# A three-stage chain (decayed attention, dense layer, routed experts) on one core: late tiles of 64 + 64 rows from two experts

## The chip, the cores and the metric

One Trainium2 chip, of which the program uses one core. The metric is the device time of one execution in microseconds (us). Engines are named as in the profile: PE (TensorE matmul), PEld (its weight load), DVE (VectorE), ACT (ScalarE), POOL (GpSimd), SP (SyncE, here the queue that starts most DMAs).

## The reference, cut to what matters

```python
state = gamma * state + einsum('bhd,bhe->bhde', k[:, :, t], v[:, :, t])     # attention, 768 steps
y[:, :, t] = einsum('bhd,bhde->bhe', q[:, :, t], state) / sqrt(D)
...
h = x @ w_in                                       # 3072 x 512 by 512 x 2048
x = (maximum(h, 0) + log1p(exp(-abs(h)))) @ w_out
...
expert_idx = argmax(x @ w_gate, axis=1)            # 8 experts, one per token
for e in range(E):
    mask = expert_idx == e
    h = maximum(x[mask] @ w1[e], 0)                # 512 x 1024
    out[mask] = gate_w[mask, None] * (h @ w2[e])   # 1024 x 512
```

For the inputs that setup_inputs() draws the eight experts get, from the largest to the smallest, 1441, 647, 291, 270, 230, 89, 74 and 30 of the 3072 tokens.

## The kernel before, in words

All matmul operands are f16. A number is held as a high and a low half, and a product is three matmuls (high by high, high by low, low by high). Attention and the dense layer run first, mixed with each other. The kernel then forms the experts' work as **slots** of 128 token rows. Experts are taken in **turns** by size, turn 0 being the largest. A slot holds rows of one turn only, so each turn's last slot is partly empty.

A table in DRAM lists each expert's tokens in the order in which they were routed; `rank` scatters into it. `early_pick` takes four early slots (j = -4 to -1) from turns 0 and 1 before all tokens are routed. After the last tokens `slots_pick` (on DVE) counts each turn's blocks of 128 rows and computes where each of the remaining slots starts; `fetch` (POOL) reads their token lists from the table, and `spread` transposes them on PE and copies them to `idsT` and `gateT`. `NSURE` late slots always run, and an If behind them runs the others up to `NSLOT` when the flag `more` is set. With the counts above the late slots are 8, 6, 3, 3, 2, 1, 1 and 1 by turn, 25 in all, which is NSURE.

A slot's steps: `gather(j)` (POOL) collects its 128 rows from `x2d`; `turn(j)` transposes them into xT by DMA on SP; `layer1(j)` is 24 matmuls of 512 columns on PE in two halves (12 each), each half followed by r and hb on ACT (lines 381 and 383) and the low half of hb on DVE (384); then a DMA transpose of hb into hT on SP (386); `layer2(j)` is 24 more matmuls; DVE scales and POOL scatters the rows to the output (398, 399). In the main loop layer2(j - 2) follows layer1(j). PE's order is written by hand.

Weights: `ring` has four parts, each one expert's w1 (half 0) and w2 (half 1). `Direct` loads the first four experts in 32 units of 512 KB (`raw`, six buffers) and splits each into high and low on ACT (133) and DVE (134) in the same stretch in which the early slots run. The loads' and the splits' places are positions counted in PE matmuls. The other four experts are split earlier and kept in `wsp`; `load_next` copies 2 MB halves of them into the ring part that the preceding turn has left, when turn 1, 2, 3 or 4 begins. It is issued for every slot with a condition `go`, and its three register values are read by SP (408 to 410).

`in_line` fixes the order of SP's DMAs in the late part as the order in which the code calls them. A list `ticks` says after which matmul of the early slots the helper steps are called: 42 `rank`, 44 `slots_pick`, 116 `spread`, the gathers of slots 0 to 2 and the turns of slots 0 and 1.

Of the kernel before, what the change touches and what calls it, by code (L numbers as in the profile page):

```python
# [8 lines left out]
F32 = mybir.dt.float32  # L9
# [11 lines left out]
P = 128  # L21
# [4 lines left out]
E = 8  # L26
# [10 lines left out]
NSLOT = NT // P + E - 1  # L37
NSURE = 25
RING = 4
TROWS = E * NT + 32 * P  # L40
# [18 lines left out]
def moe_chain(ctx, tc, q, k, v, moe_w_in, moe_w_out, moe2_w_gate, moe2_w1, moe2_w2, cst, cst16, out, dbg=None):  # L59
# [28 lines left out]
    for n in (16, 4, 8, P, E, E, 1, 32, NT // P):  # L88
        cols.append(cs[:, at0:at0 + n])
        at0 += n  # L90
    dec, zd, zd8, mask, rev, base, iota_p, iota_j, tok = cols
# [25 lines left out]
    halved = []  # L117
# [18 lines left out]
    class Direct:  # L136
# [13 lines left out]
        def at(self, pos, after):  # L150
# [8 lines left out]
            while self.m < self.n and self.SPLIT[self.m] <= pos:  # L159
# [14 lines left out]
    idsE = const.tile([P, NEARLY], U32, name="idsE")  # L174
    gateE = const.tile([P, NEARLY], F32, name="gateE")
    rg = const.tile([1, 3, 32], U32, name="rg")
# [7 lines left out]
    nblk = const.tile([P, 1], F32, name="nblk")  # L184
    cc = [const.tile([P, 2 * E], F32, name="c%d" % i) for i in range(4)]
    late = []

    def reclaim(x):

        tc.add_manual_dep(nc.gpsimd.drain().ins, x.name, NOSYNC, reason="order")  # L190
# [6 lines left out]
    def fetch(n, blk_u):  # L197
        nc.gpsimd.indirect_dma_start(
            out=late[1][0:n].rearrange("p r c -> p (r c)"), out_offset=None, in_=table.rearrange("(b r) c -> b (r c)", r=P),
            in_offset=bass.IndirectOffsetOnAxis(ap=blk_u[0:n, :], axis=0), bounds_check=TROWS // P - 1, oob_is_err=True)  # L200

    def spread(n, ids, gates):
        ps = ps_at.tile([P, 2, 32], F32, tag="at", name="idt")
        for i in range(2):
            nc.tensor.transpose(ps[:, i, 0:n], late[1][0:n, :, i], ident[0:n, 0:n])
        nc.vector.tensor_copy(out=ids, in_=ps[:, 0, 0:n])
        nc.vector.tensor_copy(out=gates, in_=ps[:, 1, 0:n])
# [7 lines left out]
    def turns_pick():  # L215
# [14 lines left out]
        nc.vector.tensor_scalar(out=kblk, in0=expert, scalar1=float(NT // P), scalar2=None, op0=ALU.mult)  # L230
        nc.vector.memset(taken, 0.0)
        nc.vector.memset(nblk, float(E * NT // P))
# [3 lines left out]
    def early_pick():  # L236
        ps = counts()
        t = r_p.tile([P, E, E], F32, tag="byt", name="byt", bufs=1)
        ns = r_p.tile([P, E], F32, tag="start", name="ns")
# [3 lines left out]
        ab32 = r_p.tile([P, 2], U32, tag="ab32", name="ab32", bufs=1)  # L243
        ab = r_p.tile([P, 2], F32, tag="ab", name="ab", bufs=1)
        a, b = ab[:, 0:1], ab[:, 1:2]
        nc.vector.tensor_copy(out=ab32, in_=ns[:, 0:2])
        nc.vector.tensor_scalar(out=ab32, in0=ab32, scalar1=7, scalar2=None, op0=ALU.logical_shift_right)
        nc.vector.tensor_scalar(out=ab, in0=ab32, scalar1=float(NEARLY), scalar2=None, op0=ALU.min)
        nc.vector.tensor_scalar(out=b, in0=b, scalar1=a, scalar2=float(NEARLY), op0=ALU.add, op1=ALU.min)
        d = r_p.tile([P, 2], F32, tag="pm", name="d")  # L250
        c = r_p.tile([P, 2], F32, tag="blk2", name="c", bufs=1)
        blk = r_p.tile([P, 1], F32, tag="blk", name="blk")
        blk_u = r_p.tile([P, 1], U32, tag="blku", name="blku")

        nc.vector.scalar_tensor_tensor(out=d[:, 0:1], in0=kblk[:, 1:2], scalar=kblk[:, 0:1], in1=a, op0=ALU.subtract, op1=ALU.subtract)
        nc.vector.scalar_tensor_tensor(out=d[:, 1:2], in0=a, scalar=kblk[:, 1:2], in1=nblk, op0=ALU.subtract, op1=ALU.add)
# [4 lines left out]
        fetch(NEARLY, blk_u)  # L261
        nc.vector.tensor_scalar(out=rP, in0=iota_j[0:1, 0:NEARLY], scalar1=a[0:1], scalar2=RING - 1.0, op0=ALU.is_lt, op1=ALU.mult)
        nc.vector.tensor_copy(out=taken[:, 0:1], in_=a)
        nc.vector.tensor_tensor(out=taken[:, 1:2], in0=b, in1=a, op=ALU.subtract)
        nc.vector.tensor_tensor(out=kblk, in0=kblk, in1=taken, op=ALU.add)
        nc.vector.tensor_scalar(out=taken, in0=taken, scalar1=-float(P), scalar2=P - 1.0, op0=ALU.mult, op1=ALU.add)

    def early_spread():
        spread(NEARLY, idsE, gateE)

    def slots_pick():
# [5 lines left out]
        n32 = r_p.tile([P, E], U32, tag="n32", name="n32")  # L277
        nc.vector.tensor_tensor(out=n32, in0=n, in1=taken, op=ALU.add)
        nc.vector.tensor_scalar(out=n32, in0=n32, scalar1=7, scalar2=None, op0=ALU.logical_shift_right)
        sl_ = cc[0][:, E:]  # L280
        nc.vector.tensor_scalar(out=sl_, in0=n32, scalar1=1.0, scalar2=None, op0=ALU.max)
# [4 lines left out]
        start = r_p.tile([P, E], F32, tag="start", name="start")  # L286
        v = r_p.tile([P, E], F32, tag="v", name="v", bufs=1)
        cmp_ = r_p.tile([P, 2, E], F32, tag="cmp", name="cmp", bufs=1)
        nc.vector.tensor_tensor(out=start, in0=end, in1=sl_, op=ALU.subtract)
        nc.vector.tensor_tensor(out=v, in0=kblk, in1=start, op=ALU.subtract)  # L290
        nc.vector.scalar_tensor_tensor(out=cmp_[:, 0], in0=start, scalar=iota_p, in1=v, op0=ALU.is_le, op1=ALU.mult)
        nc.vector.scalar_tensor_tensor(out=cmp_[:, 1], in0=end, scalar=iota_p, in1=v, op0=ALU.is_le, op1=ALU.mult)
        nc.vector.tensor_tensor(out=v, in0=cmp_[:, 0], in1=cmp_[:, 1], op=ALU.subtract)
# [821 lines left out]
```

## Time and profile before

| what | us |
|---|---|
| median of 3 runs | 942.48 (938.41 to 943.27) |
| the profiled execution | 941.44 |
| its span (first to last instruction) | 939.7 |
| PE busy in the span | 905.8 |
| first matmul of the early slots, last slot's output scatter issued | 615.7, 934.7 |

The profile is of one execution. Every stretch of the late part has its own limit, so it is read in two pieces: from 615 to 695 us, where the early slots run beside the last loads and splits, and from 695 us to the end, where slots follow each other.

### The profile page before, as it was taken

The page shows a single profiled execution, that of the slowest core. Times are in us where ns is not written, and L with a number is a line of the kernel's source. Part 1 is how long each engine was busy: PE and PEld are TensorE (multiplying, and loading weights), DVE is VectorE, ACT ScalarE, POOL GpSimd, SP SyncE. Part 2 cuts the span into 40 slices and gives each one's busy share as a digit, 9 for nine tenths or more (in the row PEclk, how much of TensorE's full clock was granted, in tenths as well). Part 3 has the DMA queues.
Part 4 walks back from the last instruction along what each step waited for, and adds up shares of the span by engine and source line. Part 5 has one row for each costly group of instructions (what it writes and reads, how often), then busy time and mean ns, then how long its engine had stood idle before and what let it go on. Part 6 is the DMA issues. An engine that isn't in the chain of part 4 may idle for free.

```text
span 939.7 us, 17862 instructions
## 1 busy us (share of the span) xinstructions
PE 905.8 (96%) x6123; PEld 481.7 (51%) x6123; DVE 583.0 (62%) x1144; ACT 505.8 (54%) x949; POOL 97.7 (10%) x93
## 2 busy tenths in 40 slices
PE   9878989999999999999999999999789999999997
PEld 6654555555555555555555555444334444444443
DVE  6799998786898897898886555664432221222211
ACT  3677877665776776777776555443442222222220
POOL 0000000010010010010010011112222211221111
PEclk9999999999999999999999999999899999999999
DMA  9983885569799799799564236878997697789971
GB/s 243 224 247 70 187 186 131 119 119 140 175 228 222 196 204 245 196 210 240 163 165 145 68 91 152 219 155 194 258 217 153 165 220 163 209 201 239 269 178 42
DMA packets 300843, 170.28 MB, mean 181 GB/s; under 512 B 262147, under 2 KB 270727, under 8 KB 299730
## 3 DMA queue, kind: packets, MB, share of 16 engines
q1 hardware_dynamic: 295170, 155.13, 70.2%
q0 software_dynamic: 5584, 13.96, 4.9%
q8 instruction: 56, 0.92, 0.4%
q14 instruction: 33, 0.27, 0.1%
HBM read 181.90 MB, written 30.93 MB: 226 GB/s over the span
## 4 chain that ended last, share of the span: by engine, by line
PE 67%; DVE 13%; issue 7%; DMA 7%; SPq 3%; POOLq 1%; POOL 0%; ACT 0%
PE bank L740 24%; PE bank L353 10%; PE h L353 9%; PE bank L703 7%; PE bank L705 7%; PE bank L704 7%; DMA raw<-in_moe_w_dram 2%; SPq L529 2%; PE psY L630 2%; DVE ring L477 2%; DVE r L719 1%; DVE ring L722 1%; DVE raw L471 1%; DVE t L469 1%; POOLq L190 1%
## 5 line engine op out<-in xcount | busy, mean ns | idle before, releaser
L740 PE MATMUL bank<-ring 128*128 128x512 f16 x1104 | 257.9, 380 | 3.4 <-DVE ring L477 3.4
L740 PEld LDWEIGHTS <-ring 128*128 128x128 f16 x1152 | 109.5, 98 | 125.0 <-issue 4.2
L705 PE MATMUL bank<-xt,ring 128*128 128x384 f16 x512 | 167.8, 328 | 4.3 <-DVE ring L477 4.3
L703 PE MATMUL bank<-xt,ring 128*128 128x384 f16 x512 | 167.7, 328 | 3.0 <-ACT ring L476 3.0
L704 PE MATMUL bank<-xt,ring 128*128 128x384 f16 x512 | 167.6, 327 | 1.4 <-DVE xt L682 1.4
L353 PE MATMUL bank<-ring,hT 128*128 x696 | 158.5, 386 | 8.3 <-DMA hT<-hb 8.3
L353 PE MATMUL h<-ring,xT 128*128 x696 | 155.3, 379 | 0.9 <-ACT r L381 0.9
L381 ACT ACTIVATE r<-h 128x512 f32<-128x512 f32 x58 | 34.6, 596 | 179.2 <-PE h L353 153.4
L353 PEld LDWEIGHTS <-hT 128*128 128x128 f16 x696 | 69.1, 99 | 93.8 <-DMA hT<-hb 9.1
L384 DVE TENSOR_TENSOR hb<-r,hb 128x512 f16<-128x512 f32 x58 | 40.2, 692 | 115.5 <-ACT hb L383 109.2
L712 ACT ACTIVATE a<-bank 128x384 f32<-128x384 f32 x128 | 62.3, 487 | 90.0 <-PE bank L705 89.8
L353 PEld LDWEIGHTS <-xT 128*128 128x128 f16 x696 | 67.8, 98 | 82.1 <-issue 1.3
L721 ACT ACTIVATE ring<-r 128x384 f16<-128x384 f32 x128 | 66.4, 519 | 54.7 <-DVE r L719 52.5
L828 POOL DMA_INDIRECT table<-row,pos x24 | 29.3, 1220 | 566.7 <-DVE pos L811 533.6
L719 DVE SCALAR_TENSOR_TENSOR r<-a,r 128x384 f32<-128x384 f32 x128 | 71.1, 557 | 22.5 <-ACT a L718 21.0
L722 DVE TENSOR_TENSOR ring<-r,ring 128x384 f16<-128x384 f32 x128 | 71.1, 556 | 19.6 <-ACT ring L721 19.4
L716 DVE TENSOR_SCALAR r<-bank 128x384 f32<-128x384 f32 x96 | 53.4, 556 | 41.0 <-ACT a L712 39.7
L705 PEld LDWEIGHTS <-ring 128*128 128x128 f16 x512 | 50.2, 98 | 40.7 <-DVE ring L477 5.9
L703 PEld LDWEIGHTS <-ring 128*128 128x128 f16 x512 | 50.1, 98 | 39.9 <-ACT ring L476 4.0
L398 DVE TENSOR_SCALAR o<-bank,gateT 128x512 f32<-128x512 f32 x25 | 18.8, 751 | 82.5 <-PE bank L353 82.5
L704 PEld LDWEIGHTS <-ring 128*128 128x128 f16 x512 | 50.2, 98 | 35.3 <-issue 0.3
L718 ACT ACTIVATE a<-a 128x384 f32<-128x384 f32 x128 | 66.7, 521 | 2.8
(185 smaller groups left out, 1074.0 us busy)
## 6 DMA issues: line engine op xcount, KB each, us to landing
ring<-wsp SPq DMA_DIRECT2D x50, 2048.0 KB
raw<-in_moe_w_dram SPq DMA_DIRECT2D x64, 512.0 KB
wsp<-hl SPq DMA_DIRECT2D x32, 512.0 KB
ring<-in_moe_w_in_dram SPq DMA_DIRECT2D x16, 512.0 KB
raw<-in_moe_w_out_dram SPq DMA_DIRECT2D x16, 512.0 KB
x2d<-xr SPq DMA_DIRECT2D x24, 256.0 KB
qkv<-in_q_dram SPq DMA_DIRECT2D x18, 256.0 KB
qkv<-in_k_dram SPq DMA_DIRECT2D x18, 256.0 KB
```

The costliest lines, as they stand in the source:

```text
L353: ins = nc.tensor.matmul(ps, lhsT=lhsT, rhs=rhs, start=start, stop=stop).ins
L384: nc.vector.tensor_tensor(out=hb[:, 1, hs], in0=r32, in1=hb[:, 0, hs], op=ALU.subtract)
L703: nc.tensor.matmul(ps, lhsT=w0[:, 0, kk, fs], rhs=xh[:, kk, :], start=(kk == 0), stop=False)
L704: nc.tensor.matmul(ps, lhsT=w0[:, 0, kk, fs], rhs=xl[:, kk, :], start=False, stop=False)
L705: now[0] = nc.tensor.matmul(ps, lhsT=w0[:, 1, kk, fs], rhs=xh[:, kk, :], start=False, stop=(kk == 3)).ins
L712: nc.scalar.activation(out=a, in_=ps, func=AF.Abs, scale=C1)
L716: nc.vector.tensor_scalar(out=r, in0=ps, scalar1=C1 * SG, scalar2=0.0, op0=ALU.mult, op1=ALU.max)
L718: nc.scalar.activation(out=a, in_=a, func=AF.Ln, bias=1.0)
L719: nc.vector.scalar_tensor_tensor(out=r, in0=a, scalar=SG, in1=r, op0=ALU.mult, op1=ALU.add)
L721: nc.scalar.activation(out=hi, in_=r, func=AF.Copy)
L722: nc.vector.tensor_tensor(out=lo, in0=r, in1=hi, op=ALU.subtract)
L740: last[0] = nc.tensor.matmul(l2[t], lhsT=gt[j][:, g, kk, t * P:(t + 1) * P], rhs=w1t[:, w, kk, :], start=(kk == 0 and p == 0), stop=(kk == ...
```

## The change

- Three late slots (`MIX` = 3, 4, 5) may be mixed: rows 0 to 63 belong to turn 1, 2 or 3 and rows 64 to 127 to turn 0. Each of their 48 matmuls becomes two of 64 output rows, with the weights of two ring parts; the second part's number is a constant (turn 0's part).
- The table is read in blocks of 64 rows, 100 rows of indices in place of 31, and each turn's rest is counted in halves. With the counts above the late slots become 9, 5, 2, 2, 2, 1, 1 and 1, 23 in all, and `NSURE` becomes 23. An If of more slots stays behind, one slot after the other.
- `keep_ahead` records r, hb, the spread's copies and others, and a later split may not be put ahead of the last four of them on ACT or DVE.
- `ticks`: rank at 48, slots_pick at 50 (with priority), register values for SP at 100, spread and gathers at 130, the turns of slots 0 and 1 at 132. In the main loop turn(j + 2) is called behind layer1(j) in place of ahead of it. `read_next` reads SP's registers one slot at a time. `load_next` begins at slot 6.

```diff
-NSURE = 25
+MIX = (3, 4, 5)
+NSURE = 23
...
+    def keep_ahead(act=None, dve=None):
+        for eng, x in ((nc.scalar, act), (nc.vector, dve)):
+            if x is not None:
+                behind[eng.engine].append(x.ins.name)
...
-                for x, y in zip(split_unit(self.raw.pop(self.m), *hl), halved):
+                for x, eng in zip(split_unit(self.raw.pop(self.m), *hl), (nc.scalar, nc.vector)):
                     tc.add_manual_dep(x, after.name, NOSYNC, reason="order")
-                    tc.add_manual_dep(x, y.name, NOSYNC, reason="order")
+                    for y in behind[eng.engine][-4:]:
+                        tc.add_manual_dep(x, y, NOSYNC, reason="order")
...
+        nc.vector.tensor_scalar(out=n32, in0=n32, scalar1=6, scalar2=None, op0=ALU.logical_shift_right)
+        nc.vector.tensor_scalar(out=odd32, in0=n32[:, 1:4], scalar1=1, scalar2=None, op0=ALU.bitwise_and)
...
         nc.vector.tensor_scalar(out=more, in0=end[0:1, E - 1:E], scalar1=float(NSURE), scalar2=None, op0=ALU.is_gt)
...
         def mm(self, j, half, ps, lhsT, w, start, stop):
-            rhs = ring[:, bass.ds(self.reg[j], 1), w, :].rearrange("p a m -> p (a m)")
-            ins = nc.tensor.matmul(ps, lhsT=lhsT, rhs=rhs, start=start, stop=stop).ins
...
+            sides = [(slice(0, HP), self.reg[j]), (slice(HP, P), RING - 1)] if j in MIX else [(slice(0, P), self.reg[j])]
+            for o, part in sides:
+                rhs = ring[:, bass.ds(part, 1), w, :].rearrange("p a m -> p (a m)")
+                ins = nc.tensor.matmul(ps[o, :], lhsT=lhsT[:, o], rhs=rhs, start=start, stop=stop).ins
...
+                keep_ahead(hi, lo)
...
+        def read_next(self, p):
...
+            for row, at_, top in ((1, p, E - RING - 1), (2, p, 1), (0, p - 1, RING - 1)):
+                ins, val = nc.values_load_multi_w_load_instructions(
...
-            left = list(range(NPL)) if 0 < p <= last_p else []
+            left = list(range(NPL)) if MIX[-1] < p <= last_p else []
...
-            ticks = {8: tick_by(3), 26: tick_by(1), 28: lambda: sl.turn(-1), 42: tick_by(2), 44: lead, 116: go}
+            ticks = {8: tick_by(3), 26: tick_by(1), 28: lambda: sl.turn(-1), 48: tick_by(2), 50: lead, 100: regs, 130: go, 132: turns}
...
-                if j + 2 < NSURE:
+                if j == 0:
                     sl.turn(j + 2)
                 hook = sl.pieces(j - LAG, 1)
                 if j < NSURE:
                     sl.layer1(j, early(hook) if j < 4 else hook)
...
+                if 0 < j < NSURE - 2:
+                    sl.turn(j + 2)
                 if j >= LAG:
                     sl.layer2(j - LAG, early(sl.pieces(j + 1, 0)) if j < 4 else sl.pieces(j + 1, 0))
```

The order of the instructions is shown at three places. The first is SP behind layer1(-1). xT_8026 and xT_8028 are the transposes of slots 0 and 1, hT_8038 is that of slot -1, raw are weight units; before:

```order
L344 DMA_TRANSPOSE xT_8026<-xg_8014 128x8x128
L344 DMA_TRANSPOSE xT_8028<-xg_8018 128x8x128
L386 DMA_TRANSPOSE hT_8038<-hb_7976 128x16x128
L127 DMA raw_8043<-in_moe2_w1_dram 128x1024
L127 DMA raw_8060<-in_moe2_w1_dram 128x1024
L127 DMA raw_8082<-in_moe2_w1_dram 128x1024
```

On SP of the changed kernel the same transposes are hT_8077 (slot -1), xT_8114 and xT_8116 (slots 0 and 1):

```order
L443 DMA_TRANSPOSE hT_8077<-hb_8009 128x16x128
L137 DMA raw_8082<-in_moe2_w1_dram 128x1024
L396 DMA_TRANSPOSE xT_8114<-xg_8100 128x8x128
L396 DMA_TRANSPOSE xT_8116<-xg_8104 128x8x128
L137 DMA raw_8122<-in_moe2_w1_dram 128x1024
```

The transpose of slot -1 moved ahead of those of slots 0 and 1, and one weight unit now also stands ahead of them.

The second is ACT at layer1(0); hb_8165 is slot 0's hidden rows, and a row with raw is a split; before:

```order
L381 ACTIVATE r32_8183<-h_8166 128x512
L133 ACTIVATE ring_88<-raw_8138 128x1024
L383 ACTIVATE hb_8165<-r32_8183 128x512
L133 ACTIVATE ring_88<-raw_8178 128x1024
L381 ACTIVATE r32_8204<-h_8187 128x512
L133 ACTIVATE ring_88<-raw_8200 128x1024
L383 ACTIVATE hb_8165<-r32_8204 128x512
```

On ACT of the changed kernel hb_8226 is slot 0's:

```order
L435 ACTIVATE r32_8244<-h_8227 128x512
L437 ACTIVATE hb_8226<-r32_8244 128x512
L143 ACTIVATE ring_88<-raw_8161 128x1024
L435 ACTIVATE r32_8265<-h_8248 128x512
L437 ACTIVATE hb_8226<-r32_8265 128x512
L143 ACTIVATE ring_88<-raw_8183 128x1024
```

Between the first r and the last hb of the slot there is one split in place of three.

The third is PE at the start of layer1(3), the first mixed slot of the changed kernel (an ISA row sets the register for the address of the row behind it):

```order
L408 MATMUL bank_71<-ring,hT 128x512
L424 TENSOR_LOAD rg
L424 ISA x2
L408 LDWEIGHTS xT
L408 ISA
L408 MATMUL h<-ring,xT 64x512
L408 LDWEIGHTS xT
L408 MATMUL h<-ring,xT 64x512
```

Where one load of weights and one matmul of 128 rows stood, there are two of 64, and only the first of the two has a register to set.

## Rows read from the trace of the kernel before

**Rows 1.** The page: its span, and busy time by engine.
```profile
span 939.7 us, 17862 instructions
PE 905.8 (96%) x6123; PEld 481.7 (51%) x6123; DVE 583.0 (62%) x1144; ACT 505.8 (54%) x949; POOL 97.7 (10%) x93
```

**Rows 2.** Groups from 600 us on: busy and mean, then idle before them.
```profile
L353 PE MATMUL bank<-ring,hT 128*128 x696 | 158.5, 386 | 8.3 <-DMA hT<-hb 8.3
L353 PE MATMUL h<-ring,xT 128*128 x696 | 155.3, 379 | 0.9 <-ACT r L381 0.9
```

**Rows 3.** Busy us by stretch; last the granted clock, DMA share, GB/s.
```profile
615.00:695.00 80.00, 68.80 (x321) 30.25 (x319) 38.84 (x81) 36.01 (x49) 19.26 (x15) 0.94 0.83 194
695.00:930.00 235.00, 235.00 (x1090) 106.53 (x1089) 51.89 (x71) 55.19 (x90) 44.18 (x42) 1.00 0.78 193
```

**Rows 4.** The chain that ended last: start, length; one of 28 like it.
```profile
695.19 5.18 PE h L353 x24
```

**Rows 5.** What PE waited for from 612 us on: total, times, longest.
```profile
PE bank L353 <- DMA hT<-hb: 8.3, 2, 5.9
PE rk L805 <- DVE oh L795: 1.4, 1, 1.4
PE h L353 <- ACT r L381: 0.9, 1, 0.9
```

**Rows 6.** Timeline around the longer wait: start, length, what, idle before.
```profile
646.01 1.06 ACT L133 ACTIVATE ring<-raw 128x1024 f16<-128x1024 f32 x1 [3.55 <-DMA raw<-in_moe_w_dram]
646.98 0.58 ACT L381 ACTIVATE r<-h 128x512 f32<-128x512 f32 x1
...
648.70 1.99 POOL L335 DMA_INDIRECT xg<-x2d,idsT  x1 [3.01 <-DVE gateT L207]
...
651.75 0.69 DVE L384 TENSOR_TENSOR hb<-r,hb 128x512 f16<-128x512 f32 x1 [0.25 <-ACT hb L383]
...
653.03 3.36 SPq L344 DMA_TRANSPOSE xT<-xg  x2
656.50 2.82 SPq L386 DMA_TRANSPOSE hT<-hb  x1
...
662.49 7.83 PE L353 MATMUL bank<-ring,hT 128*128 x24 [5.86 <-DMA hT<-hb]
```

**Rows 7.** Timeline around the shorter wait, and one undisturbed layer behind it.
```profile
678.47 1.06 ACT L133 ACTIVATE ring<-raw 128x1024 f16<-128x1024 f32 x1 [3.46 <-DMA raw<-in_moe_w_dram]
...
683.70 1.73 SPq L386 DMA_TRANSPOSE hT<-hb  x1
...
688.31 6.87 PE L353 MATMUL bank<-ring,hT 128*128 x24 [2.46 <-DMA hT<-hb]
...
695.02 5.34 PE L353 MATMUL h<-ring,xT 128*128 x24
```

**Rows 8.** PE in attention, f16; 128*64 is a tile of 64 output rows.
```profile
110.15 0.19 PE L658 MATMUL z<-vh,ring 128*128 128x64 f16 x1
110.18 0.19 PE L659 MATMUL z<-ring 128*128 128x64 f16 x1
110.30 0.32 PE L661 MATMUL z<-vh,ring 128*64 128x64 f16 x8
110.55 0.39 PE L740 MATMUL bank<-ring 128*128 128x512 f16 x1
```

**Rows 9.** PE in the first attention chunks, f32, and f16 ahead of them.
```profile
13.20 1.14 PE L891 MATMUL bank<-ring 128*128 128x384 f16 x6
14.26 1.09 PE L637 MATMUL psY<-ring 128*64 128x128 f32 x16
...
19.29 1.04 PE L572 MATMUL psT<-ident,ring 128*128 128x128 f32 x8
```

**Rows 10.** Stretches without and with copies of experts into the ring.
```profile
720.00:740.00 20.00, 20.00 (x95) 9.06 (x93) 4.09 (x6) 4.39 (x8) 4.06 (x4) 1.00 0.58 132
740.00:920.00 180.00, 180.00 (x836) 81.58 (x835) 37.69 (x53) 43.42 (x71) 31.02 (x31) 1.00 0.80 206
```

More of the change, by code (lines that the diff above doesn't have):

```diff
@@ L195, in counts, with fetch, spread @@
         return ps
-    def fetch(n, blk_u):
+    def fetch(n, blk_u, rows):
         nc.gpsimd.indirect_dma_start(
[L199 to L203, printed above, removed]
+            out=late[1][0:n, 0:rows].rearrange("p r c -> p (r c)"), out_offset=None, in_=table.rearrange("(b r) c -> b (r c)", r=rows),
+            in_offset=bass.IndirectOffsetOnAxis(ap=blk_u[0:n, :], axis=0), bounds_check=TROWS // rows - 1, oob_is_err=True)
+    def spread(n, rows, ids, gates):
+        ps = ps_at.tile([P, 2, NSLOT], F32, tag="at", name="idt")
         for i in range(2):
-            nc.tensor.transpose(ps[:, i, 0:n], late[1][0:n, :, i], ident[0:n, 0:n])
-        nc.vector.tensor_copy(out=ids, in_=ps[:, 0, 0:n])
-        nc.vector.tensor_copy(out=gates, in_=ps[:, 1, 0:n])
+            for at_ in range(0, P, rows):
+                b = slice(at_, at_ + n)
+                nc.tensor.matmul(ps[at_:at_ + rows, i, 0:n], lhsT=late[1][b, 0:rows, i], rhs=ident[b, b], start=True, stop=True)
+        keep_ahead(dve=nc.vector.tensor_copy(out=ids, in_=ps[:, 0, 0:n]))
+        keep_ahead(dve=nc.vector.tensor_copy(out=gates, in_=ps[:, 1, 0:n]))
     def by_turn(out, x):
@@ L249, in early_pick @@
[L249 to L256, printed above, removed]
+        nc.vector.tensor_scalar(out=a, in0=ab32[:, 0:1], scalar1=float(NEARLY), scalar2=None, op0=ALU.min)
@@ L289, in slots_pick @@
         nc.vector.tensor_tensor(out=start, in0=end, in1=sl_, op=ALU.subtract)
[L290 to L293, printed above, removed]
-        blk = r_p.tile([P, 1], F32, tag="blk", name="blk")
@@ L295, in slots_pick @@
-        nc.vector.tensor_reduce(out=blk, in_=v, axis=AX.X, op=ALU.add)
-        blk_u = r_p.tile([P, 1], U32, tag="blku", name="blku")
-        nc.vector.tensor_tensor(out=blk_u, in0=blk, in1=iota_p, op=ALU.add)
-        fetch(NSLOT, blk_u)
+        nc.vector.scalar_tensor_tensor(out=v, in0=start, scalar=-2.0, in1=khalf, op0=ALU.mult, op1=ALU.add)
+        nc.vector.tensor_tensor(out=v[:, 1:4], in0=v[:, 1:4], in1=odd, op=ALU.add)
+        nc.vector.tensor_tensor(out=nodd[:, 1:2], in0=nodd[:, 0:1], in1=given_of, op=ALU.min)
@@ L402, in layer2 @@
                 reclaim(x)
+        def read_next(self, p):
+            if ("s", p) in self.reg or p >= NSLOT:
+                return
+            vals = []
+            for row, at_, top in ((1, p, E - RING - 1), (2, p, 1), (0, p - 1, RING - 1)):
+                ins, val = nc.values_load_multi_w_load_instructions(
+                    rg[0:1, row, at_:at_ + 1], engines=[nc.sync.engine], min_val=0, max_val=top,
+                    skip_runtime_bounds_check_because="differences and clamped values of counts in order")
+                in_line(ins[0].ins)
+                vals.append(val[0])
+            self.reg["s", p] = vals
         def load_next(self, p, half, piece):
@@ L421, in load_next @@
             reads.append(ins)
+            if half == 0 and p < NSURE:
+                self.read_next(p + 1)
         def pieces(self, p, half, last_p=NSURE):
             AT_ = ((9,), (0,))
-            left = list(range(NPL)) if 0 < p <= last_p else []
+            left = list(range(NPL)) if MIX[-1] < p <= last_p else []
             cnt = [0]
@@ L1001, in lead, with regs, turns @@
             def lead():
-                slots_pick()
+                with tc.high_priority(offset=300):
+                    slots_pick()
             def go():
-                spread(NSLOT, idsT, gateT)
+                spread(NSLOT, HP, idsT, gateT)
                 for j in range(3):
                     sl.gather(j)
+            def regs():
+                for p in range(MIX[-1] + 1, MIX[-1] + 4):
+                    sl.read_next(p)
+            def turns():
                 for j in range(2):
@@ L1056, in moe_chain @@
                 sl.turn(j)
-            for j in range(NSURE, NSLOT):
                 sl.layer1(j)
                 rest(sl.pieces(j + 1, 0, last_p))
-            for j in range(NSURE, NSLOT):
                 sl.layer2(j)
```

169 lines of the change are left out of this document (112 added, 57 removed).

## The prediction, made before the changed kernel ran

> **What bounds the kernel now.** First the page: PE is busy 905.8 us of 939.7 [rows 1], so only less PE work or shorter PE waits can bring much. Second the groups from 600 us on: the slots are two groups of 696 matmuls [rows 2], 1392 in all, which is 29 slots of 48 (four early, 25 late). Third the table by stretch: from 695 us on PE is busy in every microsecond, at full clock, while from 615 to 695 us it lacks 11.2 of 80 us and the granted clock is 0.94 on average [rows 3]. So there are two different limits: behind 695 us the count of slots, ahead of it the waits. The chain shows the first one as layers of 5.18 us without a gap [rows 4]; a slot is two layers, 10.36 us.
>
> The waits of the first stretch are few [rows 5]: 8.3 us in two waits for hT, 1.4 us at rank, 0.9 us for a buffer. Each long wait costs more than its idle time, since the matmuls behind it run slower: 7.83 and 6.87 us for 24 [rows 6, 7] where an undisturbed layer shows 5.34 [rows 7], so 2.5 and 1.5 us more. With 11.2 us idle the loss is about 15.2 us.
>
> **What each wait hangs on.** The longer one (5.9 us): hT of slot -1. Its hb was complete at 652.4 (651.75 + 0.69), but SP started the transpose at 656.50, since the transposes of slots 0 and 1 stood ahead of it and the first of these began only at 653.03; PE had the data at 662.49 [rows 6]. The hb itself was late too: ACT reached its first r at 646.98, behind a split that had waited 3.55 us for its weights [rows 6]. The shorter one (2.5 us): hT of slot 0, started at 683.70. Three splits stood between the r and hb rows of that slot on ACT (the order shows them), and one of them had waited 3.46 us for its weights [rows 7]. Those weights were themselves queued on SP behind the same two transposes.
>
> **The change, part by part.** The sum starts from the profiled execution, 941.4 us, which is 1.0 us below the median of 942.5.
>
> 1. *Two slots fewer.* The drawn counts fill 9 + 5 + 2 + 2 + 2 + 1 + 1 + 1 = 23 late slots, exactly NSURE, so the flag `more` stays 0. PE has nothing to hide in the second stretch [rows 3], so the slots come off in full: 2 x 10.36 = 20.7 us.
>
> 2. *Mixed matmuls.* Three slots x 48 = 144 matmuls become 144 pairs of 64 output rows and 512 columns. If a pair ran one after the other, it would cost another 5.18 / 24 = 0.216 us each. Attention already has such pairs. In f16, eight half tiles (four pairs) take 0.32 us in all, 0.19 of it the length of the last, so their starts lie within 0.13 us [rows 8]; four full tiles of the same 64 columns, 0.03 apart [rows 8], start within 0.09. In f32, 16 half tiles take 1.09 us where 8 full tiles of equal columns take 1.04 [rows 9]. So halves overlap, and a pair costs at most some 0.01 us over a single one. I take 0.004 us, as the f32 rows give 0.05 / 8 = 0.006 and the reading has steps of 0.01: 0.6 us (0 to 1.4). The page TensorE: Matmul & The Clock Gate of the Trainium skill, Part 3 (Measured speedup vs the span model), gives 2.38 for three column tiles; at that efficiency of 0.79 a pair would take 0.272 us, an estimate of 8.1 us for 144, which speaks against the change, and the rows do not show such a loss.
>  Changing between full and half tiles costs too. From the last full tile to the first half tile 0.12 us pass instead of 0.03, and 0.12 to 0.13 back (110.30 + 0.32 - 0.19 = 110.43 to 110.55) [rows 8]. Behind 384 columns it is the same: the last of six starts at about 14.00 and the half tile at 14.26, 0.26 instead of 0.16 [rows 9]. So 0.1 us a change. The order of layers is 3m 1 4m 2 5m 3m 6 4m 7 5m (m mixed, the first of each pair layer1, the second layer2), ten changes: 1.0 us (up to 1.6, if the engine must empty: a matmul lasts 0.38 us [rows 2] and the next starts 0.216 behind it, so 0.164 each). The Trainium skill, TensorEngine Tiling (Array Packing), Key Properties, says that a change of tiling mode drains the engine; by that it is the 1.6, and the rows, with 0.1 us each, show less.
>  Only the first matmul of a pair sets a register, so the sequencer has as many of these as before. Sum of this part: +1.6, from 0 to 3.
>
> 3. *The order on SP.* hT of slot -1 now stands ahead of the transposes of slots 0 and 1, and its hb waits for one split instead of three. layer1(-1) ends two layers, 10.4 us, ahead of layer2(-1). Of these r, hb and its low half take some 2 (0.58 to 0.69 each), and hT arrives 6 us behind its start (656.50 to 662.49) [rows 6]: 8 of 10.4, so this wait goes, 5.9 + 2.5 = 8.4 us. What is late next is slot 0's xT: its gather starts 14 matmuls later than before. The gather takes 4.3 us (648.70 to the transpose at 653.03) [rows 6], the copies ahead of it some 0.5, the transpose about 6 as hT's; layer1(0) stands at matmul 192, 62 behind the spread or 13.4 us, so some 2.5 us are to spare. If that cover is gone, the wait is repeated there at 1 us for each us.
>
> 4. *Splits behind r and hb.* Slot 0's hb has one split between its halves in place of three, and on SP the 2.82 us of hT(-1) [rows 6] no longer stand between the transposes of slots 0 and 1 and the weights. The second wait (2.5 + 1.5 us) should go but for about 1.
>
> 5. *rank at 48.* The 1.4 us wait at rank has 6 matmuls (1.3 us) more cover, but slots_pick is 20 DVE instructions longer and stands ahead of hb of layer1(-2); fetch waits for the scatters anyway. I count 1 us gained, and 2 us left. Parts 3 to 5: 8.4 + 3 + 1 = 12.4 us, bounded by 0 and 15.2.
>
> 6. *The late copies.* Copies of 4 MB begin with turns 1 to 4, at slots 9, 14, 16 and 18 in place of 8, 14, 17 and 20. Without copies the DMA engines are busy 58%, with eight halves in 180 us 80% [rows 10]; so a half takes 0.22 x 180 / 8 = 5.0 us of all engines, and a slot by itself 0.58 x 10.36 = 6.0. Where two halves now fall into two slots twice running, 22 us are wanted of 20.7. Transposes lie in the same queue, and turn(j + 2) now stands behind hT(j): ahead of its use there were four layers, 20.7 us, and now there are three less some 5 us for hb and the start of hT, 10. I take 1 us (0 to 11, below).
>
> Table blocks, pads and SP's register reads lie beside PE's continuous work: SP's two transposes a slot take 1.7 to 3.5 us each [rows 6, 7], so at least 3 us of its 10.36 are free; were they not, a read would delay a transpose that has 10 us of slack.
>
> Sum: 941.4 - 20.7 + 1.6 - 12.4 + 1.0 = 910.9, so **911 us**.
>
> **The rivals.**
> - *The reorder does little.* The same weights arrive through the same DMA engines, already busy 83% in that stretch [rows 3]; 12 us less time for the same bytes asks for 0.83 x 80 / 68 = 98%. Then the waits move to the splits, and only some 3 of the 12.4 us come: 920. For it speaks the share; against it, that SP held the weights back behind the transposes [rows 6], so that part of the wait was not the engines'. Chance 0.18.
> - *The late copies bite.* A transpose behind two halves waits 10 us and then takes 3 itself, against a slack of 10; twice 3 us of wait, and 2.5 us for slower matmuls behind each [rows 6], 11 in place of 1: 921. For it speaks that the engines are wanted for 22 us of 20.7; against it, that before PE lost nothing where two halves followed each other at slots 16 and 19 [rows 3]. Chance 0.14.
> - *Pairs overlap in part.* If the 0.04 us by which four pairs exceed four singles [rows 8] grows with the columns, a pair takes a third more, 0.07 us, 10 us in all: 920. The f32 rows speak against it. Chance 0.05.
> - *The halves don't overlap at 512 columns:* +144 x 0.216 = 31.1 in place of 0.6: 941, no change. Nothing in rows 8 and 9 has 512 columns in halves. Chance 0.03.
> - *Slower: the If.* 23 slots of 23 are full. If 31 more rows fell to turn 0 than I count, a 24th slot would be needed, the flag would rise, and all 13 slots of the If would run: at least 13 x 10.36 = 135 us more, 1046. Close calls of argmax are too few for it. Chance 0.02.
>
> **How the numbers follow.** The likeliest case (0.58) is 911, by itself 905 to 917 (all waits gone and the pairs free: 941.4 - 20.7 - 15.2 = 905.5). The range of 905 to 924 takes in the first three rivals and leaves out the last two and 0.1 for sums of these. About 0.5%, 4.7 us, is what can be told from no change. Faster by more needs less than 937.8: all but the last two rivals, 0.94; within 0.5%: 0.03; slower: 0.03.
>
> **What would show it.** The groups of slots: 54 layers, of which 6 consist of matmuls on 128*64 tiles, 288 of them, a mixed layer 5.3 to 5.4 us long; 10.5 would mean no overlap. The waits of PE: hT should fall from 8.3 us to under 2, and the clock of the first stretch rise to 0.98 or more. From the first mixed slot to the end PE should be busy throughout; a wait for xT or hT between slots 16 and 20 would be the late copies. Wrong would make it above all a new wait of several us at layer1(0), for xT or the splits.

## The result, and the profile after

The changed kernel took 917.79 us (median of 4 runs, 912.56 to 921.52) against 942.56 us of the kernel before (938.41 to 943.27): a ratio of 0.9735, with a 95% interval from 0.9693 to 0.9776. The forecast was 911 us with a range of 905 to 924. A second set of six runs gave 918.88 us (917.29 to 921.38; ratio 0.9745, 0.9722 to 0.9768). The profile below is of the fastest of the first four, 912.56 us.

The page of the changed kernel, its span and PE's busy time, to be held against [rows 1]:

```profile
span 910.6 us, 17595 instructions
PE 882.0 (97%) x6179; PEld 473.9 (52%) x6179; DVE 581.4 (64%) x1163; ACT 500.9 (55%) x941; POOL 90.1 (10%) x89
```

The slots' matmuls by shape from 590 us on (busy and mean ns, then idle time ahead of them and its cause), to be held against [rows 2]:

```profile
L408 PE MATMUL h<-ring,xT 128*128 x576 | 128.4, 379 | 4.2 <-DMA xT<-xg 3.1 <-ACT ring L143 1.1
L408 PE MATMUL bank<-ring,hT 128*128 x576 | 127.8, 379 | 0.8 <-DMA hT<-hb 0.8
L408 PE MATMUL h<-ring,xT 128*64 128x512 f16 x72 | 16.1, 380 | 0.0
L408 PE MATMUL bank<-ring,hT 128*64 x72 | 16.1, 380 | 0.0
```

Two more groups of 72 like the last two make 288 matmuls on half tiles, that is 144 pairs. With 1152 full ones this is 27 slots of 48, as forecast. The wait for hT fell from 8.3 us to 0.8. A new one stands in the first row: 3.1 us for xT.

The same two stretches as in [rows 3], by window (busy us of PE, PEld, DVE, ACT and POOL; then granted clock, DMA share, GB/s):

```profile
615.00:695.00 80.00, 76.25 (x413) 35.55 (x413) 47.47 (x108) 39.29 (x54) 18.39 (x17) 1.00 0.96 227
695.00:900.00 205.00, 201.92 (x1044) 92.24 (x1041) 41.36 (x58) 46.61 (x76) 36.69 (x35) 1.00 0.80 197
```

In the first stretch PE now lacks 3.75 us where it lacked 11.2, and its clock is full (0.94 before). DMA moves 227 GB/s there in place of 194, at a share of 0.96, so more of the bytes fall into these 80 us. The second stretch, which lost nothing before, now lacks 3.1 us.

PE's waits from 600 us on in the changed kernel (total, times, longest), where [rows 5] stood before:

```profile
PE h L408 <- DMA xT<-xg: 3.1, 1, 3.1
PE h L408 <- DVE o L455: 1.3, 1, 1.3
PE h L408 <- ACT ring L143: 1.1, 1, 1.1
PE bank L408 <- DMA hT<-hb: 0.8, 1, 0.8
PE cnt L204 <- DVE cum L888: 0.5, 1, 0.5
```

The mixed layers in the timeline of PE (start, length to the last end, what):

```profile
703.41 5.37 PE L408 MATMUL h<-ring,xT 128*64 x48
708.62 5.35 PE L408 MATMUL bank<-ring,hT 128*64 x48
713.89 5.35 PE L408 MATMUL h<-ring,xT 128*128 x24
719.18 5.37 PE L408 MATMUL bank<-ring,hT 128*64 x48
```

Start to start, the first of these layers takes 5.21 us (a mixed one with a mixed one behind it), against 5.18 of a plain layer [rows 4]. So 24 pairs cost 0.03 us together. Where the tile changes at a layer's end, it takes 5.27 to 5.31, so a change costs about 0.1 us.

And the place of the new wait, in the timeline of SP's queue, POOL and PE (an SPq row is the time in which SP is busy starting the DMA, not its landing):

```profile
825.35 8.18 SPq L443 DMA_TRANSPOSE hT<-hb  x1
...
841.89 2.81 SPq L482 DMA_DIRECT2D ring<-wsp  x2
843.86 5.34 PE L408 MATMUL bank<-ring,hT 128*128 x24
846.07 11.82 SPq L443 DMA_TRANSPOSE hT<-hb  x1
...
854.22 5.34 PE L408 MATMUL bank<-ring,hT 128*128 x24
858.01 2.56 SPq L396 DMA_TRANSPOSE xT<-xg  x1
...
862.64 5.34 PE L408 MATMUL h<-ring,xT 128*128 x24 [3.08 <-DMA xT<-xg]
```

Two halves of copies, w1 for slot 22 and w2 for slot 21, are started at 841.9 and 844.4 us. Behind them SP needs 11.82 us to start the transpose of slot 18's hb. Of the other transposes of hb behind 700 us, that of slot 16 also stands behind two halves and takes 8.18 us, with no wait of PE after it; those behind one half take 3.05 to 6.75, and those with none directly ahead 1.5 to 2.8. The transpose of slot 20's xT is next in the queue, begins at 858.01 and comes 3.08 us late for layer1(20), which would have begun at 854.22 + 5.18 = 859.40.

### The profile page after: what moved, and what is told of

Read it like the earlier page. It is cut to its first block, busy times and chain, and to the rows that moved or that the text cites. A ratio compares the mean times of both kernels' runs of the same rounds, so it can differ in the third digit from the quotient of the medians.

```text
span 910.6 us, 17595 instructions
## 1 busy us (share of the span) xinstructions
PE 882.0 (97%) x6179; PEld 473.9 (52%) x6179; DVE 581.4 (64%) x1163; ACT 500.9 (55%) x941; POOL 90.1 (10%) x89
## 5 line engine op out<-in xcount | busy, mean ns | idle before, releaser
L408 PE MATMUL h<-ring,xT 128*128 (+1 forms) x720 | 144.5, 379 | 5.5 <-DMA xT<-xg 3.1
L408 PE MATMUL bank<-ring,hT 128*128 (+1 forms) x720 | 143.9, 379 | 0.8 <-DMA hT<-hb 0.8
L435 ACT ACTIVATE r<-h 128x512 f32<-128x512 f32 x54 | 32.1, 595 | 166.9 <-PE h L408 160.6
L438 DVE TENSOR_TENSOR hb<-r,hb 128x512 f16<-128x512 f32 x54 | 37.4, 692 | 108.9 <-ACT hb L437 108.8
L408 PEld LDWEIGHTS <-xT 128*128 128x128 f16 (+1 forms) x720 | 64.6, 100 | 80.7 <-DMA xT<-xg 3.5
L408 PEld LDWEIGHTS <-hT 128*128 128x128 f16 (+1 forms) x720 | 64.1, 100 | 76.9 <-issue 1.7
L788 ACT ACTIVATE a<-a 128x384 f32<-128x384 f32 x128 | 66.8, 522 | 2.8
L787 ACT ACTIVATE a<-a 128x384 f32<-128x384 f32 x128 | 66.7, 521 | 2.1
```

Of the source, the lines that this page charges most:

```text
L408: ins = nc.tensor.matmul(ps[o, :], lhsT=lhsT[:, o], rhs=rhs, start=start, stop=stop).ins
L787: nc.scalar.activation(out=a, in_=a, func=AF.Exp, scale=-1.0)
L788: nc.scalar.activation(out=a, in_=a, func=AF.Ln, bias=1.0)
```

## The experiments

Two questions came from this. The first: the four runs lie 9 us apart, and the median 7 us above the forecast; is that the wait for xT (theory L) or the early stretch (rival E)? The second: the early stretch came out as forecast, but by which of its steps? The table holds all kernels. "Length" is from the first matmul of the early slots to the end of the last one in the profiled execution; "idle" is PE's waiting time in it, ahead of 697 us and behind.

| kernel | median us | length | idle ahead | idle behind |
|---|---|---|---|---|
| before | 942.6 | 317.76 | 11.20 | 0 |
| changed | 917.79 | 289.76 | 3.75 | 3.08 |
| changed, again (a1) | 918.88 | 297.17 | 4.44 | 7.57 |
| no copies (a2) | 912.32 | 288.53 | 4.27 | 0 |
| turn ahead (a3) | 912.14 | 287.39 | 4.04 | 0.33 |
| w2 one slot later (a4) | 912.11 | 287.51 | 4.58 | 0 |
| order alone (b1) | 933.48 | 307.98 | 5.36 | 0 |
| mixed slots alone (b2) | 918.42 | 296.63 | 8.38 | 2.33 |
| both cures (b3) | 911.23 | 287.35 | 4.50 | 0 |
| both cures, plain matmuls (b4) | 908.91 | 284.24 | 2.68 | 0 |
| SP's reads alone (c1) | 941.33 | 314.75 | 9.62 | 0 |
| cures, old split rule (c2) | 921.02 | 299.05 | 11.50 | 0.77 |
| cures, old place of turns (c3) | 917.68 | 291.46 | 5.33 | 1.36 |
| both cures, again (c4) | 910.83 | 287.23 | 4.38 | 0 |

**Where the spread comes from.** Four kernels ran on one chip: the changed one, and three ways of taking the late wait away.

The changed kernel again.

> The changed kernel as it is, once more, for its spread and a second profile. Its four times ran from 912.6 to 921.5 us. Theory L (late copies): the spread is that of the waits behind the copies of experts in slots 15 to 20, so a run of some 918 us should show 6 to 9 us of waits for xT or hT there and under 4 us of idle time ahead of them. Rival E (early stretch): the late wait stays at some 3 us and a run of 918 us shows 9 us or more of idle time and cold matmuls between 615 and 695 us.

Measured: 918.88 us, and a profile of 919.75 us. The same stretch of its timeline:

```profile
842.39 2.88 SPq L482 DMA_DIRECT2D ring<-wsp  x2
...
846.68 12.57 SPq L443 DMA_TRANSPOSE hT<-hb  x1
...
859.38 5.40 SPq L396 DMA_TRANSPOSE xT<-xg  x1
...
867.74 7.58 PE L408 MATMUL h<-ring,xT 128*128 x24 [7.57 <-DMA xT<-xg]
```

The order is the same and the starts of the copies differ by 0.5 us, but the wait is 7.57 us, and the layer behind it takes 7.58 us in place of 5.34. The late loss is 9.8 us here and 3.1 us in the first profile; ahead of it PE waits 4.44 and 3.75 us. Of the 7.4 us between the two lengths 6.7 lie at the late wait: theory L.

No copies.

```diff
-        nc.vector.tensor_tensor(out=rg[:, 2, 1:], in0=er[:, 2, 1:], in1=er[:, 3, 1:], op=ALU.mult)
+        nc.vector.memset(rg[:, 2, 1:], 0)
```

> The flag that lets a copy of an expert into the ring run is held at 0, so no weights of turns 4 to 7 are copied (their slots compute with other weights, the same instructions). Theory L: PE waits for nothing behind 690 us, the profiled time falls by the 3.1 us of the wait for xT of slot 20, the median by 3 to 8 us to some 910 to 914, and the times lie within 4 us. Rival E: the median falls by about 3 us at most and the times still lie 8 us apart.

Measured: 912.32 us (911.09 to 914.66), no wait behind 697 us. The copies cost the changed kernel 6.6 us against its second set of runs, and the times lie within 3.6 us in place of 9 (all ten runs).

The transposes ahead again.

```diff
-                if j == 0:
+                if j + 2 < NSURE:
                     sl.turn(j + 2)
...
-                if 0 < j < NSURE - 2:
-                    sl.turn(j + 2)
```

> The transpose of slot j + 2 is called ahead of layer1(j) again, as before the change, and nothing else differs. Theory L: xT of slot 20 then stands behind one half of a copy and not behind two and hT of slot 18, so it starts some 12 us earlier and its 3.1 us wait is gone; the median falls by 3 us or more, to 911 to 915. Rival: the transpose ahead of hT holds back hT and the weight units of slots 0 to 3, and 2 to 6 us come back between 660 and 690 us, so that the median stays at 916 to 920.

Measured: 912.14 us (909.71 to 916.80; ratio 0.9682, 0.9655 to 0.9709). The late wait is 0.33 us. The early stretch shows 4.04 us of idle time, so nothing came back there and that rival fell. SP still needs 11.56 and 10.20 us to start the transposes of hT of slots 16 and 18; what changed is that xT of slots 18 and 20 no longer stands behind them.

The w2 half one slot later.

```diff
-                hook = sl.pieces(j - LAG, 1)
+                hook = sl.pieces(j - LAG - 1, 1)
...
+            rest(sl.pieces(NSURE - 1, 1))
             rest(sl.pieces(NSURE, 1))
```

> The second half of each expert (w2) is copied one slot later, at the start of layer1(p + 3) in place of layer1(p + 2), so that in slots 13 to 21 no two halves follow each other within a slot. Theory L: hT of slots 16 and 18 take at most 7 us in place of 8.2 and 11.8, no wait for xT is left behind 690 us, and the median falls by 3 us or more, with times within 5 us. Rival E: the median falls by 3 us at most and the times still lie 8 us apart.

Measured: 912.11 us (911.16 to 914.11; ratio 0.9677, 0.9654 to 0.9700). Its transposes of hT in the same stretch, in the timeline of SP's queue:

```profile
838.56 4.83 SPq L443 DMA_TRANSPOSE hT<-hb  x1
...
848.92 6.32 SPq L443 DMA_TRANSPOSE hT<-hb  x1
...
859.94 7.18 SPq L443 DMA_TRANSPOSE hT<-hb  x1
```

None takes 12 us any more, and PE waits for nothing behind 697 us. All three kernels come to 912.1 to 912.3, so the late wait is worth 6.7 us in the median, and it is a matter of order, not of bytes: the last two copy the same halves. It is not all of the spread: the times lie within 3.0 us here, but 7.1 us apart with the transposes ahead, and 6.3 us apart with both cures (b3).

**Which part of the change gave what.** The order alone: the kernel before, with the split rule, the places of rank, spread and turns, and SP's reads of the changed kernel.

```diff
-            ticks = {8: tick_by(3), 26: tick_by(1), 28: lambda: sl.turn(-1), 42: tick_by(2), 44: lead, 116: go}
+            ticks = {8: tick_by(3), 26: tick_by(1), 28: lambda: sl.turn(-1), 48: tick_by(2), 50: lead, 100: regs, 130: go, 132: turns}
...
-            left = list(range(NPL)) if 0 < p <= last_p else []
+            left = list(range(NPL)) if 5 < p <= last_p else []
```

(and keep_ahead, read_next and the place of turn(j + 2) as in the change's diff)

> The kernel before with the changed kernel's order and nothing of its mixed slots: splits behind r and hb, rank at 48, spread at 130, the transposes of slots 0 and 1 at 132, turn(j + 2) behind layer1(j), register values read one slot at a time, copies from slot 6 on. 25 late slots of 128 rows. By the prediction's terms 3 to 5 this is worth 12.4 us (0 to 15.2): some 930 us, with the two waits for hT gone from the stretch of 615 to 695 us and no wait behind it, since in this kernel's turns (slots 8, 14, 17, 20) no two halves of copies follow each other directly. Rival (the reorder does little): some 939 to 940 us, with the waits moved to the splits.

Measured: 933.48 us, 9.9 us faster than before (943.41 on that chip; ratio 0.9897, 0.9873 to 0.9922). It keeps 5.36 us of idle time and no late wait. The rival (939) fell; the forecast of 12.4 was 2.5 us high.

The mixed slots alone: the changed kernel with the order of before.

```diff
-            ticks = {8: tick_by(3), 26: tick_by(1), 28: lambda: sl.turn(-1), 48: tick_by(2), 50: lead, 100: regs, 130: go, 132: turns}
+            ticks = {8: tick_by(3), 26: tick_by(1), 28: lambda: sl.turn(-1), 42: tick_by(2), 44: lead, 116: go}
```

(and the old split rule, turn(j + 2) ahead of layer1(j), SP's reads directly ahead of their copies in place of a slot earlier)

> The changed kernel with the order of before: 23 late slots of which three are mixed, but the splits' order, rank at 42, slots_pick at 44, spread, gathers and turns at 116, and turn(j + 2) ahead of layer1(j) as before. By terms 1 and 2 it is worth 20.7 less 1.6 us, so some 923 us; slots_pick is 20 DVE instructions longer and spread still at 116, which may add 1 to 4 us of wait there: 923 to 927. The two waits for hT should stand as before, some 8 us of idle time. If the two parts add up, this one and the order alone come to the changed kernel's time without its late wait, some 912 us. Rival: the gains overlap, and this kernel comes to 918 us or less.

Measured: 918.42 us (ratio 0.9733, 0.9704 to 0.9761), so 25.0 us, more than the 19 expected; with the order's 9.9 the two make 34.9, more than the 32 of the kernel with both cures. By the medians the gains overlap by some 3 us; by the lengths the two make 30.9 and the kernel with both cures 30.4, but this kernel's length has a late wait of 2.33 us in it. The timeline of PE in this kernel shows where the gains overlap:

```profile
660.59 8.17 PE L403 MATMUL bank<-ring,hT 128*128 x24 [5.12 <-DMA hT<-hb]
...
685.14 5.34 PE L403 MATMUL bank<-ring,hT 128*128 x24 [0.84 <-DMA hT<-hb]
...
875.25 5.34 PE L403 MATMUL bank<-ring,hT 128*128 x24 [2.33 <-DMA hT<-hb]
```

The first wait for hT stands as before [rows 6]. The second one, 2.46 us and 1.5 of slow matmuls before [rows 7], is 0.84 and no slow matmul, although neither the splits nor the transposes were reordered. The third is for hT of slot 18: with the old place of turn(j + 2), which left 0.33 us of late waits in a3, this profile has 2.33. What else differs on SP at the second wait: the trace of the kernel before has 37 register reads between 643 and 683 us (three rows by line; duration in ns as least, median and most, first and last start):

```profile
L409 SPq TENSOR_LOAD <-rg x13: 265/268/630, 643.0 to 683.0; - x13
L410 SPq TENSOR_LOAD <-rg x12: 262/268/529, 643.6 to 681.9; - x12
L408 SPq TENSOR_LOAD <-rg x12: 253/268/1090, 644.2 to 682.5; - x12
```

With the bounds check behind each, a read occupies SP for some 0.56 us. Since no copies start ahead of slot 6, the kernel with mixed slots alone has none of these reads there.

SP's reads alone: the kernel before, with read_next and copies from slot 6 on, and nothing else.

```diff
-                self.reg["s", p] = (nc.sync.value_load(rg[0:1, 1, p:p + 1], min_val=0, max_val=E - RING - 1),
-                                    nc.sync.value_load(rg[0:1, 2, p:p + 1], min_val=0, max_val=1),
-                                    nc.sync.value_load(rg[0:1, 0, p - 1:p], min_val=0, max_val=RING - 1))
+                self.read_next(p)
...
-            left = list(range(NPL)) if 0 < p <= last_p else []
+            left = list(range(NPL)) if 5 < p <= last_p else []
```

> The kernel before with one edit: SP reads the three register values of a copy one slot at a time and only from slot 6 on, in the queue's order, as the changed kernel does. In the trace of the kernel before SP reads 37 values between 643.0 and 683.0 us, 25 of them behind 663 us at some 0.56 us each with the bounds check, and the transpose of slot 0's hb starts 0.14 us behind the last of them, while weight units wait in the same queue. Theory Q (SP's reads): the second wait for hT (2.5 us, with 1.5 us of slow matmuls) and the splits that wait for weights ahead of it go, the first wait (5.9 us) stays: 2 to 5 us faster, some 939 us. Rival (the prediction's step 4: the splits between r and hb make that wait): under 1 us, the second wait stays at 2 us or more.

Measured: 941.33 us (ratio 0.9981, 0.9964 to 0.9999), some 2 us faster; in the trace the length falls by 3.0. The timeline of this kernel on SP and PE:

```profile
667.95 1.02 SPq L129 DMA_DIRECT2D raw<-in_moe_w_dram  x2
...
680.57 1.70 SPq L386 DMA_TRANSPOSE hT<-hb  x1
...
685.51 5.34 PE L353 MATMUL bank<-ring,hT 128*128 x24
```

The two weight units that SP started at 670.37 and 673.87 before now start at 667.95 and right behind. The transpose of slot 0 starts 3.1 us earlier than in [rows 7], though layer1(0) starts at almost the same time (669.98 us against 670.15), and PE waits for it not at all. The first wait stays, at 6.53 us. So without these reads the second wait goes, as theory Q has it, though its worth is at the low end of what was expected.

The old split rule in the kernel with both cures.

```diff
-                for x, eng in zip(split_unit(self.raw.pop(self.m), *hl), (nc.scalar, nc.vector)):
+                for x, y in zip(split_unit(self.raw.pop(self.m), *hl), halved):
                     tc.add_manual_dep(x, after.name, NOSYNC, reason="order")
-                    for y in behind[eng.engine][-4:]:
-                        tc.add_manual_dep(x, y, NOSYNC, reason="order")
+                    tc.add_manual_dep(x, y.name, NOSYNC, reason="order")
```

(with halved, as in the kernel before, the latest two rows of the dense layer's output, and no keep_ahead)

> The kernel with both cures of the late wait, and the old rule for the splits: they are kept only behind the last rows of the dense layer's output, no longer behind r, hb and the copies of spread. By the prediction's step 4 the wait for hT of slot 0 comes back with some 3 us: 914 us, with splits between r and hb of slot 0. Theory Q: 0 to 1 us, since the reads of SP are gone.

Measured: 921.02 us against 910.83 on the same chip, 10.2 us; both expectations were far too small. PE waits six times in the early stretch; the second to the fourth and the last, and what stood behind them on ACT and DVE:

```profile
645.78 0.60 ACT L430 ACTIVATE r<-h 128x512 f32<-128x512 f32 x1 [0.82 <-DVE hb L433]
...
649.97 7.03 PE L403 MATMUL bank<-ring,hT 128*128 x24 [2.16 <-DMA hT<-hb]
651.87 1.06 ACT L139 ACTIVATE ring<-raw 128x1024 f16<-128x1024 f32 x1 [5.50 <-DMA raw<-in_moe_w_dram]
652.83 0.61 ACT L432 ACTIVATE hb<-r 128x512 f16<-128x512 f32 x1
...
654.70 0.19 DVE L213 CAST idsT<-idt 128x36 uint32<-128x36 f32 x1
...
659.29 5.34 PE L403 MATMUL bank<-ring,hT 128*128 x24 [2.30 <-DMA hT<-hb]
...
666.00 10.52 PE L403 MATMUL h<-ring,xT 128*128 x48 [1.37 <-DMA xT<-xg]
...
678.38 1.06 ACT L139 ACTIVATE ring<-raw 128x1024 f16<-128x1024 f32 x1 [1.52 <-DMA raw<-in_moe_w_dram]
...
687.00 7.03 PE L403 MATMUL bank<-ring,hT 128*128 x24 [2.19 <-DMA hT<-hb]
```

Between r of slot -1 at 645.78 and its hb at 652.83 stands a split that waited 5.50 us for its weights. The copies of spread stand behind splits on DVE too, at 654.70, where the cured kernel has them at 647.15, and so do the gathers and slot 0's xT. The order of the transposes on SP is the new one here, and the waits are there all the same. The last wait is that for hT of slot 0, 2.19 us with 1.7 us of slow matmuls: splits that wait for their weights stand among r and hb of that slot again (one of them at 678.38, between its first r and its last hb), and no register reads of SP are there. So for this wait step 4 of the prediction came out, and theory Q did not.

The old place of spread and turns in the kernel with both cures.

```diff
-            ticks = {8: tick_by(3), 26: tick_by(1), 28: lambda: sl.turn(-1), 48: tick_by(2), 50: lead, 100: regs, 130: go, 132: turns}
+            ticks = {8: tick_by(3), 26: tick_by(1), 28: lambda: sl.turn(-1), 48: tick_by(2), 50: lead, 100: regs, 116: lambda: (go(), turns())}
```

> The kernel with both cures, and spread, the gathers and the transposes of slots 0 and 1 called at matmul 116 again, so that these transposes stand ahead of that of slot -1 on SP. By the prediction's step 3 the wait for hT of slot -1 comes back with 5.9 us and 2.5 us of slow matmuls: some 8 us, 919 us. Rival: that transpose was late because of the splits ahead of its r and hb (its hb was whole at 652.4 us, and layer2(-1) stood at 656.6): 2 to 4 us, and the wait for spread's table adds up to 2 us.

Measured: 917.68 us, 6.9 us slower than c4; in the trace the length grows by 4.2, 1.4 of it in two short waits behind 697 us. The waits of PE in it, and two rows of its timeline:

```profile
PE bank L408 <- DMA hT<-hb: 3.0, 3, 2.0
PE idt L217 <- DMA tb<-table,blku: 2.3, 1, 2.3
PE h L408 <- DMA ring<-wsp: 0.8, 1, 0.8
PE cnt L204 <- DVE cum L888: 0.5, 1, 0.5
```

```profile
649.26 12.06 PE L408 MATMUL bank<-ring,hT 128*128 x48
661.82 5.34 PE L408 MATMUL bank<-ring,hT 128*128 x24 [0.49 <-DMA hT<-hb]
```

The transpose of slot -1 stands behind those of slots 0 and 1 again and starts at 657.35, yet PE waits only 0.49 us for it. The wait of 2.31 us lies at spread, which reaches the table too early, and the two layers behind it take 12.06 us in place of 10.52. Without these 3.9 us layer2(-1) would have stood that much earlier and waited some 4, which is an estimate and was not run. So the early price is 2.9 us net, within the rival's 2 to 4, and it is paid at spread first. The other 2.7 us of the median are open: this profile also starts its early slots 4 us later than c4's, which the edit doesn't reach.

**What the pairs cost.** Both cures together, and the same kernel with one matmul of 128 rows in the mixed slots.

> The changed kernel with both cures of the late wait: w2 halves one slot later and turn(j + 2) ahead of layer1(j). Theory L: each cure alone took the whole late wait, so both together give no more: 911 to 913 us, times within 4 us, and no wait behind 690 us. Rival: the cures add up and the median falls to 909 us or less.

Measured: 911.23 us (ratio 0.9671, 0.9646 to 0.9696), and 910.83 us as c4. Two cures are no better than one, as theory L has it.

```diff
-            sides = [(slice(0, HP), self.reg[j]), (slice(HP, P), RING - 1)] if j in MIX else [(slice(0, P), self.reg[j])]
+            sides = [(slice(0, P), self.reg[j])]
```

> As the kernel with both cures, but the three mixed slots use one matmul of 128 rows and one part of the ring, like all others (their rows of turn 0 meet the other expert's weights). What the pairs and the changes of tile cost is the difference of the two: by the prediction's term 2 it is 1.6 us (0 to 3), by the lengths of mixed layers in the trace (5.30 where others are 5.18) 0.8 us. Rival, pairs at the efficiency that the Trainium skill states for column tiles: 8 us, so some 904 us here. Rival, switching drains: 1.6 us and more.

Measured: 908.91 us (907.05 to 911.55). The medians differ by 2.3 us and the lengths of the two profiles by 3.1, of which 1.8 is another amount of early waiting. Without idle time the lengths are 287.35 - 4.50 = 282.85 (287.23 - 4.38 = 282.85 in c4) and 284.24 - 2.68 = 281.56: the pairs and the changes of tile cost 1.3 us together. The rows of the mixed layers above say the same: 0.03 us a layer for the pairs and about 0.1 a change. Whether the mixed slots also cause the other 1.8 us of early waiting is open. Of the rivals, the 8 us fell, and by these lengths so did drains of more than 1.6.

The repeat of the cured kernel.

> The kernel with both cures of the late wait once more, on the same chip as the three above: 911 us (909 to 915), with no wait behind 690 us and about 4 us of waits ahead of it.

Measured: 910.83 us (910.46 to 913.60; ratio 0.9671, 0.9652 to 0.9690), with 4.38 us of waits ahead and none behind. Among the kernels that compute everything it has the lowest median. By the ratios to the kernel before on the same chip it is some 7 us ahead of the changed one (0.9671 and 0.9745), and cannot be told from the kernels with one cure (0.9682 and 0.9677).

## Why the prediction came out, step by step

The range held both medians. The profiled execution of 912.56 us lies 1.6 us above the forecast, but that is luck: it is the fastest of the ten runs of this kernel. The median lies 7 us above the forecast, and most of that has one cause, the late copies of step 6.

1. *Two slots fewer, -20.7.* Right: 27 slots of 48 matmuls, 5.18 us a layer.
2. *Mixed matmuls, +1.6 (0 to 3).* Right, 1.3 by the lengths. The pairs cost 0.03 us per layer, the ten changes of tile about 0.1 us each. The Trainium skill, TensorE: Matmul & The Clock Gate, Part 3 (Measured speedup vs the span model), would have made it 8 us by the estimate that the prediction gave; the pairs of 64 columns here do not show that loss. By the Trainium skill, TensorEngine Tiling (Array Packing), Key Properties, a change of tiling mode drains the engine. The prediction put that at 1.6 us for ten changes; the trace shows less, 1.3 with the pairs in it.
3. *SP's order, -8.4, and 4. splits, -3.* The sum was near by luck, since the reasons were not right. Of the 15.2 us lost in the early stretch 3.75 and 4.44 us are left in the two profiles, so steps 3 to 5 brought some 11 of the 12.4. But undoing the split rule alone costs 10.2 us, and undoing the places of spread and turns costs 2.9 us in the early stretch of its trace, most of it at spread's table. The prediction took the wait for hT of slot -1 as SP's; c2 has SP's new order and waits for that hT still, because its hb hangs on a split without weights. The split rule carried most of what was credited to SP's order. The second wait in its turn was credited to the splits alone; c1 removes it and leaves the splits' rule as it was, and c2 has it again without the reads. So it takes both: splits between r and hb, and weights that come late, which in the kernel before they did in part because of SP's 37 register reads. The prediction had put those reads "beside PE's continuous work", where they cost nothing.
5. *rank, -1 with 2 left.* The 1.4 us at rank are gone and 0.48 us at cnt have come.
6. *The late copies, +1 (0 to 11).* This is the term that was mis-sized. It measured 3.1 us in one profile and 9.8 us in the other (7.57 and 2.24 of slow matmuls), and 6.7 us by the medians of the three kernels without it. The prediction saw the mechanism (two halves in one slot twice running, and turn(j + 2) behind hT(j)) and gave xT 10 us of slack, with 5 us for hb and the start of hT. But starting hT itself takes SP 11.8 to 12.6 us there, and the next transpose begins only then (846.07 + 11.82 = 857.89, then 858.01). The slack was gone before xT started. The prediction counted 1.7 to 3.5 us of SP for a transpose, from rows of the early slots; the late slots of the kernel before already had longer ones, behind one half of a copy:

```profile
868.17 6.27 SPq L386 DMA_TRANSPOSE hT<-hb  x1
```

   The rival "the late copies bite", at 921 us and with a chance of 0.14, lies nearer to the median than the forecast's 911; it had two waits of 3 us where there is one, of 3.1 to 7.6. The Trainium skill, DMA: Bandwidth & Descriptors, Queues, rings and completion order, says that each DMA engine takes a queue's descriptors in their order; the trace agrees, with 11.82 and 8.18 us to start a transpose behind 4 MB and 1.5 to 2.8 where no copy stands directly ahead.

For the changed kernel's second profile the sum is -20.7 + 1.3 - 10.8 + 9.8 = -20.4, where its length fell by 20.6 us; for the first, -20.7 + 1.3 - 11.4 + 3.1 = -27.7, where it fell by 28.0.

What would have made it wrong, a new wait at layer1(0), did not come. Smaller ones came in the layers behind: 1.12 us at layer1(2) for a split, 0.84 at layer2(0) for hT and 1.32 at layer1(3).

## What to carry to other kernels

When work is taken out of a pipeline, what was paced by it moves closer together: for each shared queue, list which transfers now stand directly ahead of a small one that somebody waits for, and move either of the two. A releaser in the trace is the last link only; the waits "for hT" here hung on splits, these on weights, and these in part on register reads in the queue that loads them. Steps of a reordering cover for each other, so their worth is measured by undoing each in the final kernel as well as by doing it alone.

## What the runs showed of the hardware that was not expected

- The same program, with the same order on the queue and starts within 0.6 us, waited 3.08 us in one run and 7.57 in another: starting the two transposes took 11.82 and 2.56 us in the one, 12.57 and 5.40 in the other.
- A wait of 2 to 3 us may or may not slow the matmuls behind it. Layers of 5.34 us followed waits of 3.08 us (changed), 2.95 and 2.30 us (c2); layers of 7.03 us followed waits of 2.16 and 2.19 us (also c2). Behind the wait of 7.57 us the granted clock was 0.71 on average, between the levels of 1.2 and 2.4 GHz, where it was 1.00 behind that of 3.08. The windows of the two, a1 first and then the changed kernel:

```profile
867.00:876.00 9.00, 8.26 (x28) 3.39 (x29) 0.69 (x1) 1.84 (x4) 0.74 (x1) 0.71 0.65 107
```

```profile
862.00:869.00 7.00, 6.36 (x30) 3.03 (x31) 0.69 (x1) 2.17 (x4) 0.15 (x1) 1.00 0.87 121
```

- The early slots start between 614.3 and 619.0 us in the 14 profiles; three kernels with the same code up to there (b3, c4, c3) have 614.27, 615.07 and 619.00. In c3 the granted clock is 0.97 in the first 100 us, in c4 1.00. So the times of two single profiles can differ by a few us for reasons that lie ahead of the slots.
